# A fused attention and MLP kernel: the first 360 words of its work list in another order

## The chip, the cores and the metric

The kernel runs on one core of a Trainium2 chip. The metric is the device time of one execution in microseconds (us). Three runs of the kernel before took 346.78, 346.99 and 347.33 us; the median is 346.99 us.

A core has five engines that run side by side, each working through its own instructions in order: TensorE (PE, matrix products, PEld its weight loads), VectorE (DVE), ScalarE (ACT), GpSimd (POOL) and SyncE (SP), which here only starts transfers. Transfers (DMAs) started by GpSimd form one queue, those started by SyncE another. Results of TensorE land in PSUM, from where ScalarE or VectorE must copy them out ("evict" them) before TensorE can use them again.

## The reference

Batch 8, 8 heads, 576 rows, head size 64. What is computed, cut to the core:

```python
scores = np.matmul(q, k.transpose(0, 1, 3, 2)) * scale
cum = np.cumsum(np.maximum(s, 0.0), axis=-1)
scores = np.where(causal, -1e9, scores + np.minimum(-(cum_q - cum_k), 0.0))
x = softmax(scores) @ v                      # heads side by side: (8, 576, 512)
xn = (x - mean(x)) / np.sqrt(var(x) + 1e-06) * g_ln
out = x + np.maximum(xn @ w_ch1, 0.0) @ w_ch2   # 512 -> 2048 -> 512
```

## The kernel before, in words

Each batch is cut into four row tiles of 128 and a tail of 64. Three stages follow each other, and the MLP of finished batches fills TensorE between them.

Batch 0 is worked through by tiles, since its inputs arrive by tiles. Keys and queries (with the running sums of `s` as further columns) are transposed on TensorE (`T.t.g`, line 948: row tile t, head group g) and evicted (`e.t.g`, line 140 on ScalarE, 142 on VectorE); scores (`S`, lines 970 and 978) go through the exponential on ScalarE (`x`, line 987) into bf16, are multiplied with the values (`V`, line 1028) and normalised on VectorE (`N`, lines 1042 to 1053). `L` (lines 694 and 710) makes the normalised row tile, `X` and `y` transpose and evict it, `M.c.t.j` are quarter pieces of the first MLP layer (line 1072) and `r` evicts them.

Batch 1 is worked through by heads, 8 to 15. `Q.k.g` and `Q.q.g` (line 322) transpose the keys and queries of a pair of heads, two evictions each follow (`E`), then scores of a head (`s.n`, lines 390 and 398, exponentials line 401, masks on GpSimd line 410; `d.n` is the tail of two heads, masks line 440), values (`v.n`, line 583) and the normalising (`n.n`, lines 595 to 604).

From batch 2 on two heads at a time are worked through: a burst of scores `B2.n` (line 548), its exponentials `bx` (line 553), masks `bm` on GpSimd (line 492), values `Y` (line 627), `K` (lines 644 to 654). For batch 2 the keys and queries come as pairs: `O2` copies a pair into place, `F` (line 360) transposes it, `G` evicts it; `sd`, `se`, `sm` and `tk` do the same for the tails (`tk` copies tail keys on GpSimd, line 144, `sd` is line 519). `vm.b.t` (line 232) and `vo.b` (lines 244 and 245) weigh the values on GpSimd. From batch 3 on SyncE loads rows (`lr.b.t`: keys, then queries; line 205), GpSimd casts them (`cr.b.t.u`, line 217) and SyncE transposes them by DMA (`tr`, line 224). `lv.b.t` loads values (line 205). `D` is the DMA transpose of batch 1's normalised rows (line 732). `aug` and `a3` (lines 264 and 266) copy running sums into place on SyncE.

`lp.g` (line 183) are GpSimd's loads of a pair, keys and then queries. `w2.i` (line 255) and the earlier `w1` (line 252) load a quarter of the MLP weights, and line 191 the values of batches 0 and 1, all on GpSimd's queue.

`u` and `U` take the next unit of a queue of MLP work: a first-layer unit of 16 products of 128 rows or 4 products of 512 columns (lines 1072 and 761) with its relu on ScalarE (`u`) or VectorE (`U`), or a quarter of a second-layer tile (line 780, 4 products); the last quarter is followed by an addition on VectorE (line 792) and an output transfer on SyncE (line 813). The queue's order is fixed; below, `0h9` is first-layer unit 9 of batch 0, `0y1.2` quarter 2 of second-layer tile 1, `piece12` the unit for block 1, tile 2. `W.n` are n idle products (line 858).

The order of all of this is written out by hand: a string `PLAN` of 1238 words, each one step, optionally with the engine that runs it (`:A` ScalarE, `:D` VectorE, `:P` GpSimd). The kernel emits the steps in the order of the list under a manual schedule, so that each engine runs its own instructions in the list's order. Between engines only data and buffers decide. PSUM has 8 banks: until the words `to` two serve `T`, `M` and MLP units, three serve scores, two serve `V`, `X`, `Q`, `d`, `F` and `W`, and one serves `v`. Eight staging buffers serve SyncE's loads.

```python
for word in PLAN.split():
    step, _, eng = word.partition(":")
    name, *args = step.split(".")
    args = [int(c) if c.isdigit() else c for c in args]
    STEPS[name](*args, *([E[eng]] if eng else []))
```

Of the kernel before, what the change touches and what calls it, by code (L numbers as in the profile page):

```python
# [30 lines left out]
def fast_path(  # L31
# [1151 lines left out]
    def raise_flag(count, ones, n):  # L1183
# [100 lines left out]
        x.3.0.1 V.1.0 e.3.1:D qu.3 La.2 N.1.0 V.1.1 N.1.1 L.1 S.2.0.0 x.2.0.0 S.2.0.1 x.2.0.1 S.3.0.2
        x.3.0.2 X.0 y.0:A S.3.1.2 S.2.1.1 x.2.1.1 V.2.0 N.2.0 x.3.1.2 X.1 y.1:D S.3.0.0 x.3.0.0 V.2.1
        M.0.1.0 B.0.1 M.0.1.3 S.3.0.3 x.3.0.3 M.0.1.2 N.2.1 L.2 M.0.1.1 r.0.1:A M.0.0.0 M.0.0.2 Q.q.4
        B.1.1 O E.q.4.0:A M.0.0.3 E.q.4.1:A V.3.0 N.3.0 S.3.1.1 x.3.1.1 M.0.0.1 r.0.0:D S.3.1.3 S.3.1.0
        T.4.0 e.4.0:D X.2 y.2:D x.3.1.3 Q.k.4 E.k.4.0:D T.4.1 e.4.1:D x.3.1.0 S.4.0.1 x.4.0.1 S.4.0.0
# [15 lines left out]
        ga.1.2.4 la.1.4 B2.10 bx.10.0 K.9.0 bx.10.3 bx.10.4 bx.10.2 bx.10.5 cr.3.4.0 bm.10.3 bx.10.1
        Y.9.1 U K.9.1 u u tr.3.2.4 U u tr.3.4.5 bm.10.1 Y.10.1 lv.3.1 bm.10.0 B2.11 bx.11.0 bx.11.4
        lv.3.2 bx.11.5 lv.3.3 K.10.1 bm.10.2 Y.10.0 K.10.0 bm.11.2 ga.2.0.0 lv.3.4 bx.11.2 bm.11.0 La.4
        bx.11.1 u ga.2.1.2 ga.2.0.3 U u tk.3 cr.4.1.1 lr.4.2 bx.11.3 Y.11.0 K.11.0 bm.11.3 u sd.3 U
        bm.11.1 u se.3 ga.2.0.1 lr.4.3 cr.4.0.1 vm.3.1:P Y.11.1 K.11.1 lv.4.0 lv.4.1 vm.3.4:P lr.4.4 u
        ga.2.1.0 u B2.12 bx.12.0 vm.3.2:P U bx.12.4 bm.12.2 ga.2.1.1 bx.12.1 lv.4.2 ga.2.2.0 cr.4.2.1
        ga.2.2.1 ga.2.1.3 lv.4.3 la.2.0 la.2.1 cr.4.0.0 bx.12.5 bm.12.3 vm.3.3:P cr.4.1.0 ga.2.2.2  # L1310
        bx.12.3 bm.12.1 u bx.12.2 bm.12.0 u u u B2.13 bx.13.5 bx.13.1 ga.2.0.2 la.2.2 u bx.13.0 cr.4.4.0
        sm.3 bx.13.4 tr.4.0.2 ga.2.2.3 u u bx.13.3 u Y.12.0 la.2.3 Da.2.0 bx.13.2 bm.13.0 K.12.0 u u
        B2.14 cr.4.4.1 tr.4.4.5 bx.14.2 Y.12.1 K.12.1 lv.4.4 bx.14.1 bm.13.2 bx.14.3 vo.4:P bx.14.4 u u
# [30 lines left out]
        bm.25.1 u u u u cr.7.2.0 B2.26 bx.26.3 bm.25.0 vm.7.2:P bx.26.4 Y.25.0 u bx.26.2 K.25.0 cr.7.2.1
        bx.26.1 bm.26.2 u u bm.25.3 Y.25.1 bx.26.0 bx.26.5 K.25.1 ga.6.0.0 vm.7.3:P bm.26.0 B2.27
        bx.27.0 u tk.7 bx.27.4 sd.7 bx.27.3 bm.27.2 bx.27.5 u ga.6.0.3 u bm.26.3 bm.26.1 se.7 la.5.4
        tr.7.2.4 u u U Y.26.1 u U sm.7 bx.27.1 bm.27.1 Da.5.4 Y.26.0 K.26.0 bm.27.3 K.26.1 ga.6.1.2
# [234 lines left out]
```

## Time and profile before

| what | value |
|---|---|
| median of three runs | 346.99 us |
| the profiled execution, its own time | 347.05 us |
| its span, first to last instruction | 345.5 us |
| TensorE busy | 332.2 us (96%) |
| VectorE, ScalarE, GpSimd busy | 206.6, 185.4, 168.8 us |
| mean granted TensorE clock | 0.992 |
| moved by DMA | 48.59 MB |

The times of instructions are counted from the start of the span; 1.55 us of the execution lie around the span. A row of the timeline has a start, a duration, the engine and line, the operation, what it writes and reads, how many equal instructions it merges, and in brackets the idle time before it with what ended it. Products on TensorE are pipelined, and a row's duration includes the run-out of its last product; the pitch from one row's start to the next one's is what a group costs on TensorE. In the old order the words up to `Y.8.1`, the last value step in the changed part, end at about 77.7 us; after it comes the unchanged rest of the list.

### The profile page before, as it was taken

To read this page: it belongs to the slowest core of one execution; us is meant where nothing else is said; L and a number is where in the kernel's file an instruction comes from. 1 tells how busy PE (TensorE), PEld (TensorE's weight loads), DVE (VectorE), ACT (ScalarE), POOL (GpSimd) and SP (SyncE) were. 2 spreads that over 40 slices of the span, in tenths; PEclk is the share of its full clock that TensorE was granted. 3 is DMA by queue.
4 is the path that set the end of the run, shared out by engine and by line. 5 is a ranking of instruction groups with operands and counts; after the bars stand their busy time and mean duration, and the time that the engine had idled before them with its cause. 6 is when DMAs were issued, how large, how long until landed. Compare 5 with 4: busy or idle time off the path is not lost.

```text
span 345.5 us, 8016 instructions
## 1 busy us (share of the span) xinstructions
PE 332.2 (96%) x3067; PEld 185.6 (54%) x3093; DVE 206.6 (60%) x593; ACT 185.4 (54%) x343; POOL 168.8 (49%) x306
## 2 busy tenths in 40 slices
PE   5999999989999999999999999999999999999994
PEld 2998856545545555555555555554545444444443
DVE  6687798826675687556653774557448614523412
ACT  4698889677655686357636863486434204202200
POOL 8897677696577775865685377441301001000000
PEclk9899999999999999999999999999999999999998
DMA  9999999899989999998686965600420141011022
GB/s 147 185 191 174 201 194 204 191 221 237 202 197 241 224 223 196 225 216 183 154 190 176 227 112 138 139 2 2 113 71 0 23 132 46 2 76 47 0 64 65
DMA packets 147963, 48.59 MB, mean 141 GB/s; under 512 B 135281, under 2 KB 143761, under 8 KB 147921
## 3 DMA queue, kind: packets, MB, share of 16 engines
q1 hardware_dynamic: 121856, 38.34, 51.2%
q0 software_dynamic: 24304, 8.92, 21.6%
q10 hardware_dynamic: 1760, 0.79, 0.9%
q8 instruction: 25, 0.41, 0.5%
q14 instruction: 18, 0.14, 0.1%
HBM read 37.11 MB, written 9.44 MB: 135 GB/s over the span
## 4 chain that ended last, share of the span: by engine, by line
PE 82%; SPq 6%; DMA 4%; POOL 3%; DVE 2%; issue 1%; ACT 0%
PE ph L761 32%; PE py L780 32%; PE pot L627 7%; SPq L205 5%; DMA rowtmp<-in_v_dram 3%; PE sa L548 2%; PE trt L948 2%; PE sc L548 1%; PE sb L548 1%; DMA c_in<-in_s_dram 1%; POOL v_bf L232 1%; PE ph L1072 1%; PE st L970 1%; POOL kq L217 1%; PE pot L1028 1%
## 5 line engine op out<-in xcount | busy, mean ns | idle before, releaser
L780 PE MATMUL py<-w_bf,hT 128*128 128x512 bf16 (+2 forms) x583 | 128.4, 367 | 1.8 <-issue 0.3
L761 PE MATMUL ph<-xT,w_bf 128*128 128x512 bf16 x480 | 109.8, 379 | 0.0
L752 ACT ACTIVATE hT<-ph 128x512 bf16<-128x512 f32 x97 | 58.0, 602 | 82.0 <-PE ph L761 80.6
L780 PEld LDWEIGHTS <-hT 128*128 128x128 bf16 x608 | 56.1, 98 | 60.9 <-issue 0.7
L761 PEld LDWEIGHTS <-w_bf 128*128 128x128 bf16 x544 | 51.0, 98 | 56.3
L492 POOL TENSOR_SCALAR_AFFINE_SELECT er<-er 128x256 bf16<-128x256 bf16 x96 | 38.5, 415 | 61.8 <-ACT er L553 46.9
L792 DVE SCALAR_TENSOR_TENSOR yo<-py,rstd,xb 128x512 f32<-128x512 f32 x32 | 24.0, 751 | 48.5 <-PE py L780 44.2
L750 DVE TENSOR_SCALAR hT<-ph 128x512 bf16<-128x512 f32 x39 | 26.8, 690 | 27.0 <-PE ph L761 26.2
L553 ACT ACTIVATE er<-sb 128x512 bf16<-128x512 f32 x48 | 28.2, 609 | 21.1 <-PE sb L548 21.1
L553 ACT ACTIVATE er<-sa 128x512 bf16<-128x512 f32 x48 | 28.6, 608 | 13.3 <-PE sa L548 10.5
L232 POOL TENSOR_TENSOR v_bf<-rowtmp,wt 128x512 bf16<-128x512 f32 (+1 forms) x30 | 32.4, 1085 | 1.9 <-DMA rowtmp<-in_v_dram 1.8
L627 PEld LDWEIGHTS <-er 128*128 128x128 bf16 x672 | 25.7, 97 | 10.8 <-POOL er L492 1.5
L553 ACT ACTIVATE er<-sc 128x512 bf16<-128x512 f32 x48 | 28.8, 613 | 4.1 <-PE sc L548 4.1
L627 PE MATMUL pot<-v_bf,er 128*128 128x66 bf16 x672 | 28.1, 193 | 1.1 <-POOL er L492 1.0
L684 POOL TENSOR_TENSOR rstd<-rstd,mhalf 128x4 f32<-128x4 f32 (+1 forms) x8 | 8.8, 1097 | 38.8 <-DVE rstd L683 35.7
L644 DVE TENSOR_REDUCE sums<-pot 128x5 f32<-128x10 f32 x48 | 8.0, 166 | 31.2 <-PE pot L627 30.9
L710 DVE SCALAR_TENSOR_TENSOR xn<-xb,mv,gb 128x512 bf16<-128x512 f32 x28 | 25.2, 898 | 1.0
L217 POOL CAST kq<-rowtmp 128x512 bf16<-128x512 f32 (+1 forms) x30 | 20.7, 699 | 8.9 <-DMA rowtmp<-in_k_dram 8.8
L669 DVE BATCH_NORM_STATS2 stats<-xb 128x6 f32<-128x128 f32 (+1 forms) x84 | 23.8, 323 | 0.4
L647 DVE TENSOR_TENSOR xb<-pot,rinvs 128x256 f32<-128x256 f32 x48 | 20.4, 425 | 1.6
L548 PEld LDWEIGHTS <-kq 64*128 64x128 bf16 x360 | 11.2, 94 | 10.1 <-issue 4.7
L987 ACT ACTIVATE er<-st 128x512 bf16<-128x512 f32 x24 | 13.1, 604 | 3.6 <-PE st L978 2.3
(172 smaller groups left out, 394.9 us busy)
## 6 DMA issues: line engine op xcount, KB each, us to landing
out_dram<-yo SPq DMA_DIRECT2D x32, 256.0 KB
rowtmp<-in_v_dram SPq DMA_DIRECT2D x24, 256.0 KB
rowtmp<-in_k_dram SPq DMA_DIRECT2D x20, 256.0 KB
...
v_bf<-in_v_dram POOLq DMA_DIRECT2D x8, 128.0 KB, 7.7
```

The lines of the kernel that those rows point to most:

```text
L217: nc.gpsimd.tensor_copy(out=rows[b % 2][0:pn, t, u], in_=loaded.pop(("kq"[u], b, t))[0:pn])
L232: e.tensor_tensor(out=v_bf[b % 2][0:pn, t, :, 0:D], in0=loaded.pop(("v", b, t))[0:pn], in1=wt[0:pn, t, b, :].unsqueeze(2).to_broadcast([pn ...
L492: nc.gpsimd.affine_select(out=out, in_=out, compare_op=ALU.is_ge, fill=0.0, base=0, pattern=pattern, channel_multiplier=-1,)
L548: nc.tensor.matmul(a, lhsT=lhsT, rhs=rhs, start=True, stop=True)
L553: nc.scalar.activation(out=er[:, 2 * n % 4 + i, o : o + 512], in_=bank["B", n].pop((name, i)), func=ACT.Exp, scale=scale,)
L627: nc.tensor.matmul(pot[:, t, :], lhsT=cols, rhs=v_bf[b % 2][:, kb, h, :], start=(kb == 0), stop=(kb == t),)
L710: nc.vector.scalar_tensor_tensor(out=xn, in0=tiles[t], scalar=mvs[b][:, t, 0:1] if b > 0 else mean0[:, t : t + 1], in1=gb, op0=ALU.subtrac ...
L750: nc.vector.tensor_scalar_max(out=dst, in0=ph, scalar1=0.0)
L752: nc.scalar.activation(out=dst, in_=ph, func=ACT.Relu)
L761: nc.tensor.matmul(ph, lhsT=w1_bf[:, kd, fb * P : (fb + 1) * P], rhs=xT[:, :, kd, :], start=(kd == 0), stop=(kd == KD - 1),)
L780: nc.tensor.matmul(py[t], lhsT=hT[:, fb, t * P : (t + 1) * P], rhs=w2_bf[:, fb, c0:c1], start=(fb == 0), stop=(fb == FB - 1),)
L792: nc.vector.scalar_tensor_tensor(out=yo, in0=py[t], scalar=rs, in1=x[:, c0:c1], op0=ALU.mult, op1=ALU.add)
```

## The change

The first 359 words of the list stand in another order, from the word after them (`bm.9.3`) on the list is as before. No step is added or dropped. Eighteen steps change their engine: `e.0.1`, `y.1`, `r.0.0`, `E.k.4.0`, `r.0.2`, `y.3`, `E.q.5.1`, `E.k.5.1` and `E.k.6.0` go from VectorE to ScalarE; `r.0.1`, `E.q.4.1`, `E.q.5.0`, `E.q.6.0`, `E.q.6.1`, `E.q.7.0`, `E.q.7.1`, `G.k.9` and `G.q.11` go from ScalarE to VectorE. Since `u` and `U` stand elsewhere, the relus of the first 13 units are also dealt out anew: 7 on ScalarE and 6 on VectorE before, 11 and 2 after. SyncE's loads keep their order among themselves; its transpose `D` stands ahead of `lr.3.3` and `lr.3.4` instead of behind them. On GpSimd's transfer queue `lp.10` goes behind `lp.11`, `w2.2` and `w2.3`.

```diff
-        relur.1 lr.3.0 relu.0 scan.0 scan.1 cq hi.0 qu.1 hi.1 sub.0 mid.0 lo.0 relur.2 sub.1 scan.2 W.2
-        tc.0 bc.0 ck.0 T.0.1 T.0.0 mid.1 lo.1 tc.1 e.0.1:D bc.1 T.1.1 hi.2 sub.2 e.0.0:A S.0.0.0 T.1.0
-        W.1 m mid.2 lo.2 La.3 tc.2 e.1.1:D x.0.0.0 V.0.0 bc.2 e.1.0:A S.0.1.0 N.0.0 x.0.1.0 S.1.1.0
...
-        Q.q.5 r.0.2:D B.1.0 s.8 u X.3 S.4.1.0 x.4.1.0 y.3:D Sk xk E.q.5.1:D E.q.5.0:A B.0.0 B.3.0 a3 u
-        v.8 qu.4 qu.5 Q.k.5 lp.9 E.k.5.0:D u E.k.5.1:D V.4.0 N.4.0 s.9 cr.3.0.1 n.8 V.4.1 N.4.1 Q.q.6
-        E.q.6.0:A u B.2.0 d.10 s.10 wr Q.k.6 E.k.6.0:D A.0 v.9 lp.10 w2.2 lr.3.1 E.k.6.1:D n.9 u U
-        E.q.6.1:A s.11 Q.k.7 Q.q.7 E.q.7.0:A lp.11 La.6 E.k.7.0:D E.q.7.1:A U U E.k.7.1:D v.10 n.10
-        cr.3.0.0 U d.12 s.12 U v.11 n.11 ga.1.0.0 A.2 d.14 s.13 O2.k.9:A u w2.3 B.3.1 v.12 n.12 ga.1.0.3
-        s.14 O2.k.8:A A.1 me wT lv.2.0 wx vo.2:P U v.13 n.13 ga.1.1.2 s.15 cr.3.1.1 U O2.q.9:A ga.1.0.2
-        F.k.8 v.14 ga.1.0.1 F.k.9 G.k.9:A n.14 U u A.3 R vm.2.0:P lr.3.2 v.15 cr.3.2.0 O2.k.11:A lv.2.1
-        lv.2.2 vm.2.1:P G.k.8:A ga.1.1.1 u lv.2.3 u O2.q.8:A ga.1.1.3 F.q.9 G.q.9:A n.15 ga.1.2.1
-        O2.q.11:A lv.2.4 lr.3.3 cr.3.2.1 cr.3.1.0 ga.1.2.0 ga.1.1.0 ga.1.2.3 ga.1.2.2 l.0 O2.k.10:A u u
-        lr.3.4 vm.2.3:P vm.2.2:P cr.3.3.0 u F.q.8 G.q.8:A F.q.11 G.q.11:A u u O2.q.10:A F.k.10 G.k.10:A
-        F.k.11 G.k.11:A tk.2 qu.6 qu.7 l.1 l.2 l.3 u D F.q.10 G.q.10:A cr.3.3.1 vm.2.4:P to u lv.3.0
-        B2.8 bx.8.3 bx.8.0 vo.3:P bx.8.2 ga.1.0.4 u lr.4.0 lr.4.1 u ga.1.1.4 bx.8.4 bm.8.2 sd.2 se.2
-        sm.2 bx.8.5 bx.8.1 bm.8.0 bm.8.3 bm.8.1 cr.3.4.1 u tr.3.0.2 u B2.9 Y.8.0 bx.9.0 bx.9.4 Y.8.1
+        relu.0 scan.0 relur.1 O cq hi.0 scan.1 ck.0 sub.0 mid.0 lo.0 m hi.1 tc.0 bc.0 sub.1 W.2 T.0.1 relur.2
+        mid.1 scan.2 e.0.1:A lo.1 T.0.0 W.1 hi.2 tc.1 S.0.1.0 bc.1 T.1.0 e.0.0:A sub.2 T.1.1 S.0.0.0 qu.1 mid.2
+        x.0.1.0 lo.2 V.0.1 tc.2 e.1.0:A e.1.1:D S.1.1.1 x.0.0.0 x.1.1.1 qu.2 S.1.0.0 V.0.0 N.0.1 S.1.1.0 bc.2
...
+        M.0.1.1 E.q.4.1:D E.k.4.1:D x.4.0.1 x.4.1.0 U A.1 V.3.1 s.8 N.3.1 B.2.0 L.3 u B.2.1 Sk d.8 S.4.0.0 X.3
+        y.3:A r.0.1:D wr Q.q.5 E.q.5.1:A u x.4.0.0 u Q.k.5 u v.8 La.3 E.k.5.0:D B.3.1 E.q.5.0:D S.4.1.1 n.8
+        B.0.0 U xk cr.3.0.0 a3 lr.3.1 Q.k.6 E.k.5.1:A x.4.1.1 E.k.6.0:A u V.4.1 s.9 E.k.6.1:D N.4.1 V.4.0 Q.q.6
+        N.4.0 s.10 v.9 A.3 qu.3 M.0.2.0 lp.11 d.10 A.2 M.0.2.2 M.0.2.3 n.9 M.0.2.1 E.q.6.0:D s.11 u Q.k.7
+        E.q.6.1:D w2.2 d.12 s.12 r.0.2:A E.k.7.0:D Q.q.7 E.k.7.1:D O2.k.8:A v.10 u s.13 E.q.7.0:D w2.3 n.10
+        E.q.7.1:D wT v.11 lp.10 u wx n.11 lv.2.0 A.0 u d.14 ga.1.0.0 v.12 qu.4 n.12 O2.k.9:A s.14 cr.3.1.0
+        ga.1.0.3 F.k.8 v.13 u u R qu.5 n.13 ga.1.0.2 La.6 F.k.9 ga.1.1.2 s.15 v.14 u G.k.9:D ga.1.1.0 n.14 U
+        v.15 O2.q.8:A O2.q.9:A U n.15 F.q.9 qu.6 lr.3.2 O2.k.11:A vo.2:P u ga.1.2.0 ga.1.2.1 ga.1.0.1 La.2 me
+        cr.3.1.1 u l.0 O2.q.11:A F.q.8 U ga.1.1.3 ga.1.1.1 lv.2.1 l.1 lv.2.2 G.k.8:A vo.3:P ga.1.2.3 F.k.11
+        vm.2.0:P lv.2.3 l.3 u F.q.11 cr.3.0.1 lv.2.4 ga.1.2.2 l.2 G.q.11:D G.q.8:A G.q.9:A cr.3.2.0 G.k.11:A
+        O2.k.10:A D lr.3.3 lr.3.4 u F.k.10 U U O2.q.10:A G.k.10:A F.q.10 to G.q.10:A u lv.3.0 U lr.4.0 tk.2
+        vm.2.1:P B2.8 vm.2.2:P bx.8.3 u bx.8.1 vm.2.3:P sd.2 bx.8.4 vm.2.4:P bx.8.2 qu.7 se.2 u bx.8.5 sm.2
+        ga.1.0.4 u bx.8.0 bm.8.3 u bm.8.1 B2.9 bm.8.2 bm.8.0 bx.9.5 Y.8.1 ga.1.1.4 lr.4.1 cr.3.2.1 bx.9.4
+        cr.3.3.0 bx.9.0 Y.8.0 cr.3.3.1 K.8.0 tr.3.0.2 cr.3.4.1 K.8.1 bm.9.3 bx.9.2 bm.9.0 bx.9.3 bx.9.1 bm.9.1 u
```

More of the change, by code (lines that the diff above doesn't have):

```diff
@@ L1284, in fast_path @@
[L1284 to L1288, printed above, removed]
@@ L1304, in fast_path @@
[L1304 to L1308, printed above, removed]
@@ L1309, in fast_path @@
[L1309 to L1313, printed above, removed]
@@ L1344, in fast_path @@
[L1344 to L1347, printed above, removed]
-        bx.27.2 bm.27.0 vm.7.4:P ga.6.1.3 u vm.7.1:P u u Y.27.0 ga.6.1.0 B2.28 bx.28.0 ga.6.0.2 bx.28.1
@@ new lines, in fast_path @@
+        u u U ga.4.0.3 bm.19.3 bx.19.4 bm.19.2 Y.18.0 u u ga.4.0.2 u K.18.0 ga.4.1.0 bm.19.0 Y.19.0 B2.20
+        bx.20.0 vm.5.4:P ga.4.1.2 bx.20.2 lr.6.2 lr.6.3 cr.6.2.0 Y.19.1 K.19.1 K.19.0 ga.4.2.2 bx.20.3 bx.20.4
+        bm.20.2 lv.6.2 bm.20.0 ga.4.2.3 u ga.4.2.0 u vm.6.1:P bx.20.5 bm.20.3 cr.6.0.1 bx.20.1 u u u ga.4.1.1
+        bm.20.1 ga.4.0.0 Y.20.0 K.20.0 u u u u cr.6.3.1 lr.6.4 lr.7.0 cr.6.3.0 cr.6.4.0 lv.6.3 Y.20.1 ga.4.2.1
+        vo.6:P B2.21 bx.21.4 bm.21.2 lr.7.1 la.4.0 la.4.1 u bx.21.1 cr.6.1.0 ga.4.1.3 K.20.1 la.4.2 bx.21.2
@@ new lines, in fast_path @@
+        cr.7.3.1 bm.25.1 u u u u cr.7.2.0 B2.26 bx.26.3 bm.25.0 vm.7.2:P bx.26.4 Y.25.0 u bx.26.2 K.25.0
+        cr.7.2.1 bx.26.1 bm.26.2 u u bm.25.3 Y.25.1 bx.26.0 bx.26.5 K.25.1 ga.6.0.0 vm.7.3:P bm.26.0 B2.27
+        bx.27.0 u tk.7 bx.27.4 sd.7 bx.27.3 bm.27.2 bx.27.5 u ga.6.0.3 u bm.26.3 bm.26.1 se.7 la.5.4 tr.7.2.4 u
+        u U Y.26.1 u U sm.7 bx.27.1 bm.27.1 Da.5.4 Y.26.0 K.26.0 bm.27.3 K.26.1 ga.6.1.2 bx.27.2 bm.27.0
+        vm.7.4:P ga.6.1.3 u vm.7.1:P u u Y.27.0 ga.6.1.0 B2.28 bx.28.0 ga.6.0.2 bx.28.1 bx.28.3 bx.28.4 Y.27.1
@@ new lines, in fast_path @@
+        bm.30.3 bx.31.1 bm.31.1 Y.30.1 K.30.1 ga.7.1.0 ga.7.0.4 bm.31.3 ga.7.1.4 ga.7.1.3 bx.31.4 bm.31.2 u U
+        Y.31.1 U bm.31.0 ga.7.1.2 u Y.31.0 K.31.0 K.31.1 ga.7.2.2 ga.7.2.3 ga.7.2.0 u u ga.7.1.1 ga.7.2.4 u u u
+        U ga.7.0.0 u u u u ga.7.2.1 la.7.0 la.7.1 la.7.2 la.7.3 Da.7.0 u u u u u u u u u u u u u u u u u U u U u
+        la.7.4 U u U u u u u U U gd u Da.7.4 u u u u u u u u u u u u u u u u U u u u U U U u u U u U U U U fl u
+        u u u u u vl u u u u u u u u u u u u u u u u u u
```

86 lines of the change are left out of this document (42 added, 44 removed).

## The prediction, made before the change was run

> **What bounds the kernel now.** I read the page first (busy times, slices, the chain of waits), then the DMA view and one long window of the changed part.
>
> ```profile
> PE 332.2 (96%) x3067; PEld 185.6 (54%) x3093; DVE 206.6 (60%) x593; ACT 185.4 (54%) x343; POOL 168.8 (49%) x306
> PE   5999999989999999999999999999999999999994
> PE 82%; SPq 6%; DMA 4%; POOL 3%; DVE 2%; issue 1%; ACT 0%
> q0 software_dynamic: 24304, 8.92, 93.4%
> 36.20:57.20 21.00, 20.51 (x271) 13.77 (x269) 18.16 (x46) 17.95 (x36) 15.49 (x31) 1.00 1.25 198
> ```
>
> TensorE is busy in 332.2 of 345.5 us, and the chain lies on it for 82%. An order cannot shorten its products; it can only move the 13.3 us in which it is idle, and the stretches in which a group is drawn out. GpSimd's transfer queue (q0, share over the first 80 us) is taken 93.4% of that time, so its loads arrive when they arrive. VectorE and ScalarE are busy 18.16 and 17.95 of 21.0 us between 36.2 and 57.2 us: there a moved eviction can be late. So I look for the waits of TensorE up to the end of the changed part (`Y.8.1`, 77.7 us), and then for what the unchanged rest can make of a lead.
>
> **The change part by part.** *The start.* The first product of batch 0, its key row, and the first scores (timeline rows):
>
> ```profile
> 7.29 0.60 ACT L140 CAST rowb<-tiletmp 128x512 bf16<-128x512 f32 x1
> 7.42 0.88 DVE L292 TENSOR_TENSOR_SCAN c_sc<-c_one,c_sc,c_in 64x320 f32<-64x320 f32 x1 [0.57 <-ACT c_in L1222]
> 8.22 0.16 DVE L281 COPY rowb<-trc 128x24 bf16<-128x24 bf16 x1
> 8.53 1.64 PE L948 MATMUL trt<-ident,rowb 128*68 128x128 bf16 x16 [1.61 <-DVE rowb L285]
> 10.21 1.01 ACT L140 COPY kq<-trt 68x1024 bf16<-68x1024 bf16 x1 [1.42 <-PE trt L948]
> 11.56 0.31 PE L970 MATMUL st<-kq 68*128 68x128 bf16 x1
> ```
>
> `T.0.1` begins when `bc.0` (8.22) has filled the row; `bc.0` sits behind `scan.2` (0.88, after a wait of 0.57), and `ck.0` (7.29) behind `relur.2` on ScalarE. The new order has `bc.0` before `scan.2` and `ck.0` before `hi.1`. By the two durations `T.0.1` could come 0.57 + 0.88 = 1.45 earlier; for other work in between I take 1.1, so 7.4. `e.0.1`, now on ScalarE (1.01, by 10.21), follows half of the transposes, and its scores stand next: 7.4 + 0.85 + 1.0 = 9.3 instead of 11.56. Part of these 2.2 us is lost again while the inputs of the next tiles arrive; I keep 1.5 (estimate). All of it ends at a wall:
>
> ```profile
> 24.95 4.24 POOL L191 DMA_DIRECT2D v_bf<-in_v_dram  x5
> v_bf<-in_v_dram POOLq DMA_DIRECT2D x8, 128.0 KB, 7.7
> 35.53 0.90 PE L583 MATMUL pot<-v_bf,er 128*128 128x65 bf16 x15
> 36.27 0.42 PE L322 MATMUL trqk<-ident,kp 96*128 96x96 bf16 x6
> 36.52 1.06 PE L1072 MATMUL ph<-xT,w_bf 128*128 128x128 bf16 x16
> 38.92 0.76 PE L1028 MATMUL pot<-v_bf,er 128*128 128x65 bf16 x20
> ```
>
> `v.8` (35.53) needs the five value loads of batch 1. Their issue ends at 24.95 + 4.24 = 29.19, and the median to landing is 7.7, so 36.9 at the latest. Its 15 products took 0.90, where 20 of the same size at 38.92 took 0.76: at 0.04 each, the 15 are due 0.57, so some 0.3 of waiting for the last load, which I put at 36.2. Nothing ahead of these loads in GpSimd's queue changes, so the early gain is counted at nothing, and `v.8` covers it.
>
> *Term 1, 0.90.* What is done by the wall counts. The pitch of a group is its duration less the run-out: 36.27 to 36.52 is 0.25 where the row says 0.42, so 0.17. `Q.k.5` then costs 0.25, a unit such as that at 36.52 1.06 − 0.17 = 0.89, say 0.90. The new order puts `piece03`, `piece13` and `Q.k.5` ahead of `v.8`, 2.05 in all, and `M.0.2.*` (a unit, 0.90) and `S.4.1.1` (taken like `Q.k`, 0.25) behind it, 1.15. Difference 0.90 of TensorE's work, if it gets there in time: 35.53 + 0.90 − 1.5 = 34.9, before 36.2 with 1.3 to spare.
>
> *Terms 2 and 3.*
>
> ```profile
> 62.17 1.03 PE L780 MATMUL py<-w_bf,hT 128*128 128x512 bf16 x4
> 63.45 1.89 PE L780 MATMUL py<-w_bf,hT 128*128 128x512 bf16 x8 [0.25 <-DMA w_bf<-in_moe_w_ch_dram]
> 74.40 0.34 POOL L245 TENSOR_TENSOR v_bf<-wt,v_bf 128x32 bf16<-128x32 f32 x1
> 75.07 0.41 POOL L492 TENSOR_SCALAR_AFFINE_SELECT er<-er 128x256 bf16<-128x256 bf16 x1
> 75.15 0.38 PE L548 MATMUL sc<-kq 64*128 64x320 bf16 x4
> 76.51 0.60 PE L627 MATMUL pot<-v_bf,er 128*128 128x66 bf16 x14 [0.98 <-POOL er L492]
> 77.12 0.60 POOL L217 CAST kq<-rowtmp 64x512 bf16<-64x512 f32 x1
> ```
>
> Term 2, 0.42: the last second-layer weights `w2.3` arrive late. The four products at 62.17 need 1.03 − 0.17 = 0.86, so the group at 63.45 could be 62.17 + 0.86 = 63.03. `w2.3` now stands ahead of `lp.10` (two loads), and that wait goes. `lp.10` in turn is late for `O2.k.10`, which the order has at its end.
>
> Term 3, 1.38: `Y.8` (76.51) follows the burst at 75.15 + 0.22 = 75.38 only after 1.13, waiting for GpSimd's masks, and loses 0.25 more before its second half. GpSimd comes to the masks (the first at 75.07) only behind casts, weighted values and, just ahead of them, `vo.3` (74.40). The new order takes three casts behind the masks (`cr.3.2.1`, `cr.3.3.0`, `cr.3.3.1`, 0.6 each by 77.12), one cast (`cr.3.1.0`) and `vo.3` (four instructions, the longest 0.34, so at most 1.36; I take 1.1) ahead to where GpSimd has room, and one cast in (`cr.3.0.1`): 4 × 0.6 + 1.1 − 0.6 = 2.9 less, above 1.38. The wait goes; late next is the burst's exponentials.
>
> *Term 4, about −0.7.* An old wait goes, new ones come:
>
> ```profile
> 39.99 0.41 PE L322 MATMUL trqk<-ident,qp 96*128 96x96 bf16 x6 [0.31 <-DVE rinvs L595]
> 44.53 0.80 ACT L140 COPY kq<-trqk 64x576 bf16<-64x576 bf16 x1
> 46.02 0.79 DVE L142 COPY kq<-trqk 64x576 bf16<-64x576 bf16 x1
> 47.68 0.69 DVE L750 TENSOR_SCALAR hT<-ph 128x512 bf16<-128x512 f32 x1 [0.17 <-PE ph L761]
> 53.47 0.60 ACT L752 ACTIVATE hT<-ph 128x512 bf16<-128x512 f32 x1
> ```
>
> Old: `Q.q.6` (39.99) comes 1.07 after 38.92 where 0.76 − 0.17 = 0.59 would do: 0.48 lost to `n.8`, which the new order has further ahead. New: the eighteen swaps and the relus. An eviction of `E` costs ScalarE 0.80 and VectorE 0.79, a relu 0.60 and 0.69, so no step gets dearer by more than 0.1; the swaps shift load. Seven relus on ScalarE become eleven, and after what goes the other way it gains some 1.4 us in 36.2 to 57.2: 17.95 → 19.3 of 21.0. I walked the new order by hand with these durations: 0.3 at `d.12`/`Q.q.7` (banks behind `E.q.6.1`, ScalarE behind `d.12`'s exponential), 0.3 at `v.13` (behind `n.12`), 0.4 at `v.15` (a mask behind `R` and `cr.3.1.0`), 0.15 at `F.k.11`: 1.15. Net 0.48 − 1.15 = −0.67. Bounds: +0.48 if none appears, −1.8 if they double.
>
> Lead at `Y.8`: 0.90 + 0.42 + 1.38 − 0.67 = 2.0.
>
> *What the rest makes of it.* The rest is as before, but what feeds it is not:
>
> ```profile
> 65.46 1.40 SPq L205 DMA_DIRECT2D rowtmp<-in_k_dram  x1
> 68.29 0.83 DVE L710 SCALAR_TENSOR_TENSOR xn<-xb,mv,gb 128x512 bf16<-128x512 f32 x1
> 69.25 0.64 SPq L205 DMA_DIRECT2D rowtmp<-in_q_dram  x1
> 70.65 4.08 SPq L732 DMA_TRANSPOSE xT<-xn  x1
> 77.68 1.48 POOL L492 TENSOR_SCALAR_AFFINE_SELECT er<-er 128x256 bf16<-128x256 bf16 x4
> 81.14 0.58 PE L627 MATMUL pot<-v_bf,er 128*128 128x66 bf16 x14
> 90.74 0.84 POOL L144 COPY kz<-kq 64x256 bf16<-64x256 bf16 x2
> 92.90 0.40 PE L519 MATMUL sd<-kq,kz 128*128 128x64 bf16 x8
> ```
>
> `D` (70.65, holds SyncE 4.08) moves ahead of `lr.3.3` (65.46) and `lr.3.4` (ends 69.25 + 0.64). It waits for the last normalised row (old 68.29 + 0.83 = 69.12). In the new list `l.2` is the last and stands earlier; by my walk it ends near 65.9, and every load queued behind `D` waits with it: with `lr.3.3` taking 1.40 and about half of that for its second load, and `lr.3.4` two times 0.64, `lr.3.4` is issued by 66 + 4.1 + 2.1 + 1.3 = 73.5. No row shows when a SyncE load lands; old `cr.3.4.1` ran at 77.12, 7.2 after the issue at 69.25 + 0.64, so at most 7.2, and I take half, 3.6: 77.1, give or take 0.5. GpSimd's `cr.3.4.1` (0.60) needs it, and the masks `bm.9` (1.48) now stand behind that cast: done at 78.7 to 79.6, where `Y.9.0` (81.14) with the lead of 2.0 would begin at 79.1. Gain there 1.5 to 2.0. Later `sd.3` (92.90) needs the tail keys (90.74 + 0.84) behind SyncE's transposes of batch 3; SyncE works nearly without a gap from `lr.3.3` to there (an estimate: 0.3 to 0.7 earlier). 92.90 − 91.58 = 1.3 of slack, so 1.6 to 2.0 passes. I take **1.8**.
>
> Against the profiled execution, 347.05 (345.5 span and 1.55 around it): 345.25. This execution stands 0.06 above the median of 346.99, so 345.2 there. Its own range, from 1.5 less 0.6 for the walk to 2.0 plus 0.7 (two of the four new waits not coming): 344.3 to 346.1.
>
> **The rivals.** *The rest doesn't bind* (0.12): `lr.3.4` lands early, or the walk's waits don't come; and all of the lead stays, with the new waits away (2.0 to 3.2): 343.8 to 345.0. Against it: SyncE's row of transfers.
>
> *The clock* (0.08).
>
> ```profile
> 8.00:8.50 0.50, 0.00 (x0) 0.00 (x0) 0.50 (x4) 0.26 (x2) 0.50 (x1) 1.00 1.78 190
> 9.00:9.50 0.50, 0.50 (x7) 0.50 (x6) 0.14 (x1) 0.00 (x0) 0.50 (x1) 0.50 1.65 187
> 12.50:13.00 0.50, 0.45 (x9) 0.38 (x8) 0.38 (x1) 0.47 (x1) 0.32 (x2) 1.00 2.43 155
> ```
>
> The granted clock (last but two) is 1.00 while TensorE idles, 0.50 after, and 1.00 again by 12.5. Another start may keep it at half for as long again, some 3.5 us: 1.75 more, less the 1.3 to spare at `v.8`, and work that is waiting for data then; at worst 1.0 of the forecast's gain goes: 345.9 to 346.2. The Trainium skill, "TensorE: Matmul & The Clock Gate", section "What's actually happening", has a free-running window of 3413 ns after which the clock follows the activity in it, so the moment of the first products decides; the three rows agree with that. By that rule the earlier `T.0.1` could as well keep the full clock, which would end at the same wall and change nothing.
>
> *The change doesn't do it* (0.15): the swaps and relus make ScalarE late in 36 to 57, term 4 is −1.8 or worse, and the rest takes half of what is left: 346.3 to 347.7, within 0.2% (0.69 us, about what a measurement of this kernel can tell from no change).
>
> *Slower* (0.23): `D` starts late. `Y.9.0` is no earlier than before once `lr.3.4` is there only at 81.14 − 1.48 − 0.60 = 79.06, which is 2.0 above my 77.1, so with `D` at 68 or later (for instance `l.2` behind an addition of a second-layer tile on VectorE that is itself late). From there each us is a us: with `D` at the old 70.65, 4.65 above my 66, `Y.9.0` comes at 79.06 + 2.65 + 2.08 = 83.8, 2.65 later: 349.6 against the median; the bound of 7.2 for the landing, with `D` at 66, gives 80.7 + 2.08 = 82.8, 1.6 later: 348.6. So 347.7 to 349.6. For it: the old rows end at 69.12. Against it: the old `D` was held by its place behind the loads, not by the rows.
>
> **How the numbers follow.** Forecast 0.42, the rivals 0.12, 0.08, 0.15, 0.23. Faster 0.62, same 0.15, slower 0.23. The range 343.9 to 348.4 leaves out the upper half of the last. The forecast's own range is 344.3 to 346.1.
>
> **What would show it.** `T.0.1` near 7.4 and first scores near 9.3; `v.8` still ending near 36.3, drawn out by a load (wrong if it ends later or without that wait); no idle before the second-layer products near 61 to 62 for weights; `Y.8.1` first, its group ending near 75.4, with little waiting for masks; `D` at 66; `Y.9.0` at 79.2 to 79.7; a wait for `tk.3` at `sd.3`. The prediction is wrong if `D` starts after 68, if the half clock lasts beyond 13 us, or if ScalarE's queue holds scores up by more than 1.2 us in all.

## The result and the profile after

The changed kernel takes 345.02 us (median of four runs, 344.74 to 345.24) beside 346.88 us of the kernel before on the same chip: a ratio of 0.9939, interval 0.9916 to 0.9963. The prediction was 345.2. The profiled execution took 345.24 us with a span of 343.7 us, 1.8 us less than before.

The page of the changed kernel, busy times and chain:

```profile
PE 333.9 (97%) x3093; PEld 185.4 (54%) x3093; DVE 207.1 (60%) x589; ACT 186.8 (54%) x347; POOL 168.7 (49%) x306
PE 85%; POOL 7%; DVE 2%; DMA 2%; issue 1%; POOLq 0%
```

No engine's busy time moved by more than 1.7 us. The chain runs over TensorE for 85% instead of 82%; SyncE's 6% are gone from it.

Where the 1.8 us come from is seen at four places of TensorE's timeline. First the start, with the window of the granted clock (the last number but two of the window's line):

```profile
7.71 1.89 PE L948 MATMUL trt<-ident,rowb 128*68 128x128 bf16 x16
10.07 0.31 PE L970 MATMUL st<-kq 68*128 68x128 bf16 x1
9.00:9.50 0.50, 0.50 (x7) 0.50 (x6) 0.00 (x0) 0.50 (x1) 0.50 (x1) 1.00 1.94 206
```

`T.0.1` starts 0.82 earlier and the first scores 1.49 earlier. The half clock of before (0.50 in this window) does not come in this execution. Then the wall, the values of batch 1:

```profile
35.00 0.44 PE L583 MATMUL pot<-v_bf,er 128*128 128x65 bf16 x9
35.86 0.60 PE L583 MATMUL pot<-v_bf,er 128*128 128x65 bf16 x6 [0.42 <-DMA v_bf<-in_v_dram]
36.30 0.40 PE L970 MATMUL st<-kq 68*128 68x64 bf16 x8
```

TensorE reaches `v.8` at 35.00 instead of 35.53, has to wait for a load in the middle of it, and leaves it at 36.30, where it left it at 36.27 before. Behind the wall there is a wait (1.06, third row) that the kernel before does not have; TensorE's rows first, then VectorE's and GpSimd's beside them:

```profile
52.40 0.61 PE L583 MATMUL pot<-v_bf,er 128*128 128x65 bf16 x15 [0.23 <-DVE xm L604]
62.36 1.03 PE L780 MATMUL py<-w_bf,hT 128*128 128x512 bf16 x4
65.83 1.89 PE L780 MATMUL py<-w_bf,hT 128*128 128x512 bf16 x8 [1.06 <-DVE yo L792]
61.77 1.97 DVE L710 SCALAR_TENSOR_TENSOR xn<-xb,mv,gb 128x512 bf16<-128x512 f32 x1
64.24 0.75 DVE L710 SCALAR_TENSOR_TENSOR xn<-xb,mv,gb 128x512 bf16<-128x512 f32 x1
65.03 0.75 DVE L792 SCALAR_TENSOR_TENSOR yo<-py,rstd,xb 128x512 f32<-128x512 f32 x1
61.59 1.04 POOL L232 TENSOR_TENSOR v_bf<-rowtmp,wt 128x512 bf16<-128x512 f32 x1
62.58 1.62 POOL L217 CAST kq<-rowtmp 128x512 bf16<-128x512 f32 x2
```

The last quarter of second-layer tile 0 is done at 62.36 + 1.03 = 63.39; its addition on VectorE runs only at 65.03, behind `l.1` (1.97 where its neighbours take 0.75) and `l.3`. Tile 2 needs that bank and waits 1.06. Last, `Y.8` and what follows it, with SyncE's `D` and last load of `lr.3.4` and GpSimd's masks:

```profile
67.08 2.22 SPq L732 DMA_TRANSPOSE xT<-xn  x1
72.11 0.59 SPq L205 DMA_DIRECT2D rowtmp<-in_q_dram  x1
73.02 0.66 POOL L492 TENSOR_SCALAR_AFFINE_SELECT c<-c 64x512 bf16<-64x512 bf16 x1 [2.08 <-ACT c L532]
75.08 0.59 PE L627 MATMUL pot<-v_bf,er 128*128 128x66 bf16 x14
76.00 3.62 PE L761 MATMUL ph<-xT,w_bf 128*128 128x512 bf16 x16
78.31 0.77 POOL L492 TENSOR_SCALAR_AFFINE_SELECT er<-er 128x256 bf16<-128x256 bf16 x2 [0.24 <-ACT er L553]
79.45 0.58 PE L627 MATMUL pot<-v_bf,er 128*128 128x66 bf16 x14
91.21 0.40 PE L519 MATMUL sd<-kq,kz 128*128 128x64 bf16 x8
```

GpSimd now waits 2.08 ahead of its masks instead of being late with them, and `Y.8` runs without a wait. Its end, 76.00, lies 1.69 ahead of the old 77.69; `Y.9.0` (79.45) and `sd.3` (91.21) lie 1.69 ahead too.

From the end of `v.8` to the end of `Y.8` it was 77.69 − 36.27 = 41.42 and is 76.00 − 36.30 = 39.70. This length is used below. The runs below come from three chips, and loads and transposes land differently from run to run (on one of these chips the kernel before took between 345.47 and 350.52 us), but when the changed kernel was run again on another chip its length was 39.70 there too. Steps of less than 1 us are therefore read from the trace, not from the time.

### The profile page after: what moved, and what is told of

Its sections match the earlier page's. It is cut to its first block, busy times and chain, and to the rows that moved or that the text cites. A ratio compares the mean times of both kernels' runs of the same rounds, so it can differ in the third digit from the quotient of the medians.

```text
span 343.7 us, 8035 instructions
## 1 busy us (share of the span) xinstructions
PE 333.9 (97%) x3093; PEld 185.4 (54%) x3093; DVE 207.1 (60%) x589; ACT 186.8 (54%) x347; POOL 168.7 (49%) x306
## 4 chain that ended last, share of the span: by engine, by line
PE 85%; POOL 7%; DVE 2%; DMA 2%; issue 1%; POOLq 0%
PE py L780 35%; PE ph L761 34%; PE pot L627 7%; DMA v_bf<-in_v_dram 2%; POOL v_bf L191 2%; PE sa L548 2%; POOL rowb L179 2%; PE sc L548 1%; PE sb L548 1%; PE pot L583 1%; DVE xn L710 1%; POOL w_bf L252 1%; POOL kq L910 1%; DVE yo L792 0%; DVE stats L669 0%
## 5 line engine op out<-in xcount | busy, mean ns | idle before, releaser
L780 PE MATMUL py<-w_bf,hT 128*128 128x512 bf16 (+2 forms) x608 | 130.9, 368 | 1.1 <-DVE yo L792 1.1
L752 ACT ACTIVATE hT<-ph 128x512 bf16<-128x512 f32 x102 | 61.2, 604 | 80.4 <-PE ph L761 78.8
L492 POOL TENSOR_SCALAR_AFFINE_SELECT er<-er 128x256 bf16<-128x256 bf16 x96 | 37.5, 405 | 60.2 <-ACT er L553 45.1
L750 DVE TENSOR_SCALAR hT<-ph 128x512 bf16<-128x512 f32 x34 | 23.4, 690 | 25.3 <-PE ph L761 24.6
L232 POOL TENSOR_TENSOR v_bf<-rowtmp,wt 128x512 bf16<-128x512 f32 (+1 forms) x30 | 33.8, 1134 | 2.8 <-DMA rowtmp<-in_v_dram 2.7
L710 DVE SCALAR_TENSOR_TENSOR xn<-xb,mv,gb 128x512 bf16<-128x512 f32 x28 | 26.9, 960 | 1.0
L217 POOL CAST kq<-rowtmp 128x512 bf16<-128x512 f32 (+1 forms) x30 | 20.0, 681 | 6.3 <-DMA rowtmp<-in_k_dram 6.2
```

What stands on the lines that cost most here:

```text
L232: e.tensor_tensor(out=v_bf[b % 2][0:pn, t, :, 0:D], in0=loaded.pop(("v", b, t))[0:pn], in1=wt[0:pn, t, b, :].unsqueeze(2).to_broadcast([pn ...
L492: nc.gpsimd.affine_select(out=out, in_=out, compare_op=ALU.is_ge, fill=0.0, base=0, pattern=pattern, channel_multiplier=-1,)
L710: nc.vector.scalar_tensor_tensor(out=xn, in0=tiles[t], scalar=mvs[b][:, t, 0:1] if b > 0 else mean0[:, t : t + 1], in1=gb, op0=ALU.subtrac ...
L750: nc.vector.tensor_scalar_max(out=dst, in0=ph, scalar1=0.0)
L752: nc.scalar.activation(out=dst, in_=ph, func=ACT.Relu)
L780: nc.tensor.matmul(py[t], lhsT=hT[:, fb, t * P : (t + 1) * P], rhs=w2_bf[:, fb, c0:c1], start=(fb == 0), stop=(fb == FB - 1),)
```

## The experiments

Each is the changed kernel with one edit (the two versions at the end have two); ratios are to the kernel before on the same chip.

**The changed kernel again**, on the chip of the last three runs below.

> The changed kernel itself, unaltered, beside the two versions below on the same chip. Expected: 0.9939 of the kernel before within 0.003, that is 345 where the kernel before takes 347; its xn of l.1 takes 2.0 or 2.5 and the wait for the addition 1.06 or 1.6.

Measured: 346.09 us, 0.9963 (0.9943 to 0.9983); length 39.70, the addition's wait and `l.1`'s 1.97 as in the first profile. The gain holds on the other chip, at the lower end of what was measured first.

**The old start.**

```diff
- ... cq hi.0 scan.1 ck.0 sub.0 mid.0 lo.0 m hi.1 tc.0 bc.0 sub.1 W.2 T.0.1 relur.2 mid.1 scan.2 e.0.1:A
+ ... cq hi.0 scan.1 hi.1 sub.0 mid.0 lo.0 m relur.2 sub.1 scan.2 W.2 tc.0 bc.0 ck.0 T.0.1 mid.1 e.0.1:A
```

> The new list with its start put back in the old order: relur.2 and scan.2 stand ahead of ck.0 and bc.0 again. Theory (the early gain ends at v.8, which waits for the last value load landing near 36.2): T.0.1 starts near 8.5 instead of 7.71, the half clock of 8.8 to 12.2 us may come back, TensorE comes to v.8 up to 1.5 later than 35.0, v.8 ends between 36.3 and 36.9 and the time is 345.0 to 345.6, 0 to 0.6 above the changed kernel. Rival (the early gain is passed on): v.8 ends 1.5 to 2 later and the time is 346.5 to 347.

Window and `v.8` of this run:

```profile
9.00:9.50 0.50, 0.50 (x8) 0.50 (x7) 0.00 (x0) 0.00 (x0) 0.50 (x1) 0.50 1.90 194
35.35 0.66 PE L583 MATMUL pot<-v_bf,er 128*128 128x65 bf16 x15
35.85 0.40 PE L970 MATMUL st<-kq 68*128 68x64 bf16 x8
```

`T.0.1` started at 8.76 and the clock was half again. (That isn't the old start alone: the slow stretch also came in runs with the new one, see "The clock" further down.) TensorE came to `v.8` only 0.35 later than in the changed kernel; the values had landed earlier in this run, `v.8` ended at 35.85, and `Y.8` at 75.80. The time was 346.50 us (0.998, 0.9957 to 1.0003). By the ratios that is some 0.6 above the changed kernel run again and 1.4 above its first result, with intervals that overlap, so the time alone would fit the rival too; `v.8` speaks against it, since it did not end later, and the length is 39.95, 0.25 more. The start is worth little at the wall; part of its gain goes in the changed kernel's waits for row loads near 24 us (0.41 and 0.26 idle), which this run doesn't have. Clock and earlier start together weigh 0.35 there; their shares are not shown.

**Values ahead of weights.**

```diff
-    ld_w1(2)
     nc.gpsimd.memset(kq[2][:, :, :, S:SP], 0.0)
...
     for t in range(NT):
         ld_cast_v(1, t)
+    ld_w1(2)
...
- S.4.1.1 n.8 B.0.0 U xk cr.3.0.0
+ S.4.1.1 M.0.2.0 M.0.2.2 M.0.2.3 M.0.2.1 n.8 B.0.0 U xk r.0.2:A cr.3.0.0
```

> The new list with the five value loads of batch 1 ahead of the third load of first-layer weights in GpSimd's queue, and M.0.2 with its relu directly behind S.4.1.1, so that a unit without those weights stands ahead of the first that needs them. Theory (v.8 waits for values): they land some 2.5 us earlier, v.8 runs without a wait and ends near 35.6 instead of 36.30, and the time falls by 0.5 to 0.7, to 344.3 to 344.5, if nothing later takes it. Rival (the wait moves to the weights, or the masks of bm.9 hold Y.9.0): no change, 345.0.

Three rows of TensorE:

```profile
34.65 0.62 PE L583 MATMUL pot<-v_bf,er 128*128 128x65 bf16 x15
45.02 0.22 PE L426 MATMUL sd<-kq 68*128 68x64 bf16 x2 [0.40 <-DVE kq L142]
66.50 1.89 PE L780 MATMUL py<-w_bf,hT 128*128 128x512 bf16 x8 [1.61 <-DVE yo L792]
```

The wall did move: `v.8` ran without a wait and was done at 35.10, 1.20 earlier. But `v.10` came at 45.99, 0.13 later than in the changed kernel, since ScalarE's and VectorE's copies were not ready for TensorE that early (the row at 45.02 is the largest single wait), and the addition's wait grew to 1.61. The length became 41.57. The time, 346.22 us (0.9977), is close to the changed kernel's. Neither expectation named the right place: the gain was lost at the evictions, not at weights or masks. Part of that is the edit's own doing: `r.0.2` now stands ahead of `E.k.5.1` on ScalarE, and that copy began at 37.06 instead of 36.31, although the values had come earlier.

**Work put behind the wall.**

```diff
- Q.q.5 E.q.5.1:A u x.4.0.0 u Q.k.5 u v.8
+ Q.q.5 E.q.5.1:A u x.4.0.0 v.8 u Q.k.5 u
```

> The new list with two units and Q.k.5 put behind v.8 (u and Q.k.5 and u, 2.05 us of TensorE's work). Theory (term 1: what is done ahead of the wall counts, at its full length): v.8 still ends near 36.3, behind a wait of some 2.5, and everything after it comes 2.05 later: 347.0. Rival (the wall is not the load but TensorE's own work): v.8 ends 2 earlier and the time stays at 345.0.

`v.8` in this run, two of its five pieces:

```profile
34.34 0.25 PE L583 MATMUL pot<-v_bf,er 128*128 128x65 bf16 x3 [1.11 <-DMA v_bf<-in_v_dram]
...
36.16 0.19 PE L583 MATMUL pot<-v_bf,er 128*128 128x65 bf16 x1 [0.21 <-DMA v_bf<-in_v_dram]
```

TensorE comes to `v.8` at 33.00, takes its products one load at a time, and is through at 36.19: the wall is the loads. The length grew to 43.03, by 3.33: the 2.05 moved, 0.55 because the wait for the addition was 1.61, and 0.73 between `v.8` and `v.9`. 349.87 us (1.0081, 1.0048 to 1.0114): what is done ahead of the wall counts at least in full.

**lp.10 ahead of w2.2 and w2.3 again.**

> The new list with lp.10 back ahead of w2.2 in GpSimd's queue, so that w2.3 is behind two more loads again, as before the change. By the sum of the prediction (term 2) w2.3 lands 1 to 2 us later and TensorE waits 0.4 or more for it near 62 to 63, and Y.8 comes 0.4 later (measured from the end of v.8, so that another landing of the values doesn't count: 40.1 us to the end of Y.8 instead of 39.70). Rival (the wait of 1.06 for the addition at 65.83 covers it): a wait for weights of 0.3 to 1 near 62.4, and less than 0.2 lost at the end of Y.8.

The last load of `lp.9` and the load of `w2.3`, first in the kernel before, then in the changed kernel, then in this run (last number: us from issue to landing); below them this run's last quarter of tile 0, the first products that need `w2.3`:

```profile
qp<-in_q_dram POOLq DMA_DIRECT2D x1, 144.0 KB, 12.4
w_bf<-in_moe_w_ch_dram POOLq DMA_DIRECT2D x1, 512.0 KB, 10.1
qp<-in_q_dram POOLq DMA_DIRECT2D x1, 144.0 KB, 11.5
w_bf<-in_moe_w_ch_dram POOLq DMA_DIRECT2D x1, 512.0 KB, 9.8
qp<-in_q_dram POOLq DMA_DIRECT2D x1, 144.0 KB, 11.7
w_bf<-in_moe_w_ch_dram POOLq DMA_DIRECT2D x1, 512.0 KB, 11.8
62.92 1.02 PE L780 MATMUL py<-w_bf,hT 128*128 128x512 bf16 x3
```

`lp.9` was issued at 40.14, 40.12 and 40.30 and landed at 52.5, 51.6 and 52.0; `w2.3` was issued at 53.29, 50.57 and 51.13 and landed at 63.4, 60.4 and 62.9. So `w2.3` comes 10.9 behind `lp.9` in the kernel before and in this run, where `lp.10` stands between them, and 8.8 behind it in the changed kernel, whatever its own issue: `lp.10` is worth 2.1. In the changed kernel the weights are there 2.0 ahead of their products (62.36). Here they landed just as the products came, and neither the wait of the theory nor that of the rival followed. The length is 39.99, and 0.30 of it lies between `v.8` and `v.9`, far ahead of these weights (346.12 us, 0.9981, four runs).

**The casts back ahead of the masks.** `cr.3.2.1` behind `cr.3.2.0`, `cr.3.3.0` behind `vm.2.2`, `cr.3.3.1` ahead of `vm.2.4`.

> The new list with the three casts cr.3.2.1, cr.3.3.0 and cr.3.3.1 back ahead of GpSimd's masks of burst 8. Theory (term 3: the masks were late because of what GpSimd had ahead of them): cr.3.3.1 waits for its load, which D now holds back to near 73.5, the masks start near 75 instead of 73.02, Y.8 waits 1 to 2 us for masks and ends 1 to 2 us later (41 us or more from the end of v.8). Rival (GpSimd has room enough, since it idled 2.08 ahead of these masks): Y.8 within 0.2 of 39.70 from the end of v.8.

```profile
74.24 0.61 POOL L217 CAST kq<-rowtmp 128x512 bf16<-128x512 f32 x1 [5.34 <-DMA rowtmp<-in_k_dram]
78.80 0.60 PE L627 MATMUL pot<-v_bf,er 128*128 128x66 bf16 x14 [3.37 <-POOL er L492]
```

The first row is `cr.3.3.0` on GpSimd, which waits 5.34 for a row load of `lr.3.3` behind `D`; the second is `Y.8`, which waits 3.37 for the masks behind these casts, more than the 1 to 2 expected. The length is 44.07, the time 350.81 us (1.010, 1.0071 to 1.013, two runs). With `D` ahead of the loads, casts in the old places would have cost more than the whole gain. What they would cost with `D` behind the loads, as in the kernel before, this run doesn't tell.

**D behind lr.3.3 and lr.3.4.**

```diff
- O2.k.10:A D lr.3.3 lr.3.4 u F.k.10
+ O2.k.10:A lr.3.3 lr.3.4 D u F.k.10
```

> The new list with D behind lr.3.3 and lr.3.4 instead of ahead of them. Theory (the rest did not bind at Y.9.0, where the masks were done 0.37 ahead): D starts near 70.5 to 71 and lands near 75, the first unit of batch 1 behind Y.8 waits 0 to 0.3, the masks bm.9 come earlier, and the end stays within 0.3 of the changed kernel, measured from the end of v.8. Rival (D ahead was worth something): the unit behind Y.8 waits 0.5 to 1.5 for xT.

```profile
72.58 3.17 SPq L732 DMA_TRANSPOSE xT<-xn  x1
81.78 0.58 PE L627 MATMUL pot<-v_bf,er 128*128 128x66 bf16 x14
```

`D` started 5.5 later (3.2 later against `Y.8`, which itself came 2.3 later in this run), yet the unit behind `Y.8` did not wait: `Y.9.0` follows the end of `Y.8` by 3.45, as in the changed kernel. Early row loads were late in this run, so `v.8` came at 37.33; the length, 40.55, holds a wait of 1.61 for the addition and 0.30 ahead of `v.9`. 346.41 us (0.9971). The place of `D` alone is worth nothing up to `Y.9.0` here.

**The addition ahead of l.3.**

```diff
- vm.2.0:P lv.2.3 l.3 u F.q.11
+ vm.2.0:P lv.2.3 u l.3 F.q.11
```

> The new list with l.3 behind the last quarter of second-layer tile 0 instead of ahead of it, so that the tile's addition on VectorE stands ahead of l.3. Theory (the wait of 1.06 at 65.83 is the order on VectorE: the quarter ends near 63.4 and its addition runs at 65.03 behind l.1 and l.3): the addition runs near 63.95, the wait shrinks to 0.1 to 0.2 and Y.8 comes 0.9 earlier; Y.9.0 then meets the masks bm.9, done at 79.1, so 0.4 to 0.9 of it reaches the end: 344.1 to 344.6. Rival (the addition is late for another reason, or the masks take it all): 345.0.

`l.1` and the addition on VectorE, `vm.2.0` on GpSimd, and a wait of TensorE's in the rest of the list:

```profile
61.09 0.75 DVE L710 SCALAR_TENSOR_TENSOR xn<-xb,mv,gb 128x512 bf16<-128x512 f32 x1
62.83 0.75 DVE L792 SCALAR_TENSOR_TENSOR yo<-py,rstd,xb 128x512 f32<-128x512 f32 x1 [0.78 <-POOL v_bf L232]
61.60 1.14 POOL L232 TENSOR_TENSOR v_bf<-rowtmp,wt 128x512 bf16<-128x512 f32 x1 [0.62 <-DMA rowtmp<-in_v_dram]
112.12 1.04 PE L761 MATMUL ph<-xT,w_bf 128*128 128x512 bf16 x4 [0.69 <-DMA xT<-xn]
```

The wait is gone and the length is 38.49, 1.21 less. But two things differ: the addition stands ahead, and `l.1` took 0.75, because `vm.2.0` waited for its load and began behind it. And of the lead, which had grown by 1.89 at `Y.8` and `sd.3` (0.68 of it from values that landed early), 0.96 arrived at the end of the span: 0.69 went at 112 us, where batch 2's transposed rows were late. 345.74 us (0.9948, 0.992 to 0.9975).

**GpSimd away from l.1.** `vm.2.0`, `cr.3.0.1` and `cr.3.2.0` stand behind `tk.2`; VectorE's order is that of the changed kernel.

> The new list with vm.2.0, cr.3.0.1 and cr.3.2.0 behind tk.2 in GpSimd's list, so that GpSimd runs nothing next to l.1 on VectorE. VectorE's own order stays. Theory A (the xn of l.1, 1.97 instead of 0.75, was held up by GpSimd's work beside it): l.1 takes 0.75, the addition runs near 63.8 instead of 65.03 and the wait of 1.06 of TensorE near 65 is gone or under 0.2. Theory B (l.1 is slow for another reason, the order on VectorE alone makes the addition late): l.1 takes 1.5 or more again and the wait stays at 0.8 or more. What comes behind is no test of this: the loads lv.2.2 to lv.2.4 wait for the buffers that these steps free, so D and the loads of lr.3.3 and lr.3.4 come 2 to 4 us later, and Y.8 or Y.9.0 may wait up to 3 us.

`l.1` and the addition on VectorE, then `vm.2.0`, now far behind them, and `Y.8`:

```profile
60.89 0.75 DVE L710 SCALAR_TENSOR_TENSOR xn<-xb,mv,gb 128x512 bf16<-128x512 f32 x1
62.93 0.75 DVE L792 SCALAR_TENSOR_TENSOR yo<-py,rstd,xb 128x512 f32<-128x512 f32 x1
65.72 1.04 POOL L232 TENSOR_TENSOR v_bf<-rowtmp,wt 128x512 bf16<-128x512 f32 x1
73.27 0.59 PE L627 MATMUL pot<-v_bf,er 128*128 128x66 bf16 x14 [0.21 <-POOL er L492]
```

Theory A holds: with nothing on GpSimd beside it `l.1` takes 0.75, the addition runs in time, and the wait of 1.06 is gone though the order on VectorE is the same. The loads I feared for were not late. Part of it is given back at `Y.8`, which waits for masks; the length is 39.03. 345.36 us (0.9941, 0.9918 to 0.9964).

**Nine steps back on VectorE.**

> The changed kernel with the nine steps that went from VectorE to ScalarE (e.0.1, y.1, r.0.0, E.k.4.0, r.0.2, y.3, E.q.5.1, E.k.5.1, E.k.6.0) back on VectorE. Theory (term 4: the swaps alone move little, since each costs nearly the same on both engines): from the end of v.8 to the end of Y.8 within 0.3 of 39.70, less what the wait for the addition differs. Rival (the swaps carry part of the gain): 1 us or more is lost there to waits for VectorE.

One of the waits of TensorE that came with it:

```profile
41.34 0.77 PE L1028 MATMUL pot<-v_bf,er 128*128 128x65 bf16 x20 [1.51 <-DVE kq L142]
```

The rival was right. `v.8` was reached at 36.89, and the length grew to 42.77, with this wait of 1.51 for VectorE in it; 350.18 us (1.0066, 1.0028 to 1.0105). That each step costs the same on both engines says nothing about the queue that it joins. The other nine, back on ScalarE, weren't tried.

**Two versions meant to be kept.** Both move `la.2.3 Da.2.0` ahead of the units in front of them, so that SyncE issues batch 2's transpose ahead of an output transfer; one has GpSimd away from `l.1`, the other the addition ahead of `l.3`.

```diff
- tr.4.0.2 ga.2.2.3 u u bx.13.3 u Y.12.0 la.2.3 Da.2.0
+ tr.4.0.2 ga.2.2.3 la.2.3 Da.2.0 u u bx.13.3 u Y.12.0
```

> A version meant to be kept: vm.2.0, cr.3.0.1 and cr.3.2.0 behind tk.2 as in the run with GpSimd away from l.1, and la.2.3 and Da.2.0 ahead of the units in front of them, so that SyncE issues the transpose of batch 2's normalised rows 0.5 to 0.6 earlier, ahead of an output transfer. Expected: no wait for the addition near 65, no wait for xT near 112, and 1.2 to 1.6 less than the changed kernel on the same chip (some 343.6 where the kernel before takes 347). If the lead is lost again, it is at a load or transpose of SyncE behind 100 us.

> The run with the addition ahead of l.3, and la.2.3 and Da.2.0 moved ahead as in the version with GpSimd away. Expected: the wait of 0.69 for xT at 112 falls to 0.1 or less, so 0.6 to 0.9 less than with the addition alone: 1.2 to 1.8 below the changed kernel on the same chip. Rival (the transposes themselves are slow when issued close behind each other): the wait stays above 0.4.

With GpSimd away: 345.03 us, 0.9925 (0.990 to 0.9951); length 39.01, no wait for the addition or for xT. Its median is 1.06 below the changed kernel's on the same chip, near the 1.2 expected, and nine of the changed kernel's twelve runs are slower than its slowest, but the intervals of the two ratios overlap: probably better, not shown beyond doubt. With the addition ahead: 345.86 us, 0.9957 (0.9932 to 0.9981). Its length was the shortest, 38.48, and no wait for xT came at 112; the lead went earlier, at `sd.3`:

```profile
90.86 0.84 POOL L144 COPY kz<-kq 64x256 bf16<-64x256 bf16 x2 [2.96 <-DMA kq<-kq]
91.76 0.41 PE L519 MATMUL sd<-kq,kz 128*128 128x64 bf16 x8 [1.59 <-POOL kz L144]
```

The tail keys wait for SyncE's transposes and `sd.3` for the tail keys: the supply that the prediction had named. Its limit isn't a fixed time, though. Up to here the list is that of the run with the addition ahead, where a lead over the kernel before of 3.58 passed `sd.3` (89.32, no wait); here a lead of 2.90 at `Y.8` was cut to 1.14, because SyncE's transposes came later in this run.

## Why the prediction was right

*The start and the wall: right.* `T.0.1` at 7.71 (said 7.4), first scores at 10.07 (9.3), TensorE at `v.8` at 35.00 (34.9), its end at 36.30 behind a load (36.2 to 36.3). That the early gain counts for nothing holds in the run with the old start. What lay beneath was weighed wrongly: the 1.5 kept from the start is not the start's, which was worth 0.35 at `v.8`. The remainder of the 1.43 gained there (0.53 in time, 0.90 in work) came from the order between 10 and 35 us, which the prediction did not work out.

*The clock.* I had put the half clock at 0.08 as a loss, and named the other way as one that changes nothing. The changed kernel kept the full clock in its two profiles. The start of `T.0.1` does not settle it, however: with `T.0.1` at 7.76 to 8.03 the clock stayed full in five of the other runs and was half for some 3.4 us in five (with the three casts back, for instance). What separates them is how long TensorE was busy in the 3.41 us ahead, in the changed kernel and in the run with the three casts back, where the slow stretch began at 7.75:

```profile
5.40:8.81 3.41, 2.71 (x17) 1.54 (x17) 3.13 (x12) 1.51 (x5) 3.33 (x7) 1.00 1.68 194
```

```profile
4.34:7.75 3.41, 1.75 (x8) 0.45 (x6) 2.92 (x12) 1.92 (x5) 3.33 (x6) 1.00 1.57 188
```

TensorE (the second number) was busy 2.71 us of them in the one and 1.75 in the other. In all seven profiles with a slow stretch it was at most 1.94 of the 3.41 us ahead of it (1.31 in the kernel before); in the seven without it was at least 2.13 in every stretch of 3.41 us that begins between 3.5 and 7.7. The Trainium skill, "TensorE: Matmul & The Clock Gate", section "What's actually happening", has TensorE's activity in a free-running window decide. The profiles agree with it: the slow stretches begin between 7.7 and 8.8 from run to run. And it changed nothing at the wall, as said: the run with the three casts back came to `v.8` at 34.98 with the slow stretch, the changed kernel at 35.00 without.

*Term 1, 0.90: right*, measured as 0.90 less 0.03 for the wall; the run with work behind the wall lost its 2.05 and more.

*Term 2, 0.42: right.* The wait for `w2.3` is gone: it landed at 60.4 instead of 63.4. Of these 3.0 us, 2.1 are the two loads of `lp.10`, which now land behind it; by the rest, 0.9, the queue was ahead already at `lp.9`. With `lp.10` back the wait stayed away, but only just: landing and products came within 0.1 of each other, so whether the move was needed for the whole 0.42 stays open.

*Term 3, 1.38: right.* `Y.8` follows its burst without an idle time for masks, 0.09 later than the pitch alone would have it, so 1.29 came. In the kernel before GpSimd ran without a break from 65.5 to the masks, now it stands idle for 2.08 ahead of them. The casts put back brought a wait of 3.37, but through the loads that `D` holds up and not through GpSimd's work.

*Term 4, −0.67: right in sign and about in size, wrong in its places.* What the other three terms leave of the 1.72 us of length is −0.89. Of the four new waits only that at `v.13` behind `n.12` came (0.23 idle, said 0.3). Of the others, that ahead of `d.12` was 0.1 and two did not come; in their place stands the wait of 1.06 for the addition. The prediction took `xn` at its duration in the old order (0.83, begun ahead of GpSimd's next instruction); in the new order one began behind `vm.2.0` and took 1.97. The run with GpSimd away shows the cause.

*The swaps: wrong.* "No step gets dearer by more than 0.1; the swaps shift load" left out that VectorE would otherwise be late. Nine of them undone cost 3.07 of length, 0.55 or so of it at the addition. Since the terms were read as waits of the new order as it stands, the sum did not suffer.

*The rest: right that it can take some of the lead, wrong that it took any.* The lead was 1.69 at `Y.8` (said 2.0) and 1.69 at `Y.9.0`; the masks were done at 78.31 + 0.77 = 79.08, 0.37 ahead. `D` began at 67.08 (said 66), right behind the last normalised row (66.29 + 0.75), itself late by the long `l.1`; `lr.3.4` was issued by 72.70 (said 73.5). Two errors of 0.2 to 0.3 cancel in the 1.8. The mechanism is real all the same: the leads of the two runs with the addition ahead were cut at 112 and at 91.8 us, though the first had passed `sd.3` with 3.58.

*The slower rival* needed `D` at 68 or later with the loads behind it; `D` came 0.9 us short of that. With `D` behind the loads even 72.58 cost nothing, so its place ahead of them made the risk and, in that run, brought nothing.
